# The issue order of an attention and state-space kernel, from a planner's ranks to one written list

## The chip, the cores and the metric

The kernel runs on one core of one Trainium2 chip. The metric is the device time of one execution in microseconds (us). A NeuronCore has five engines, each with an instruction stream of its own that is worked off strictly in order: PE (TensorE, matmul), DVE (VectorE), ACT (ScalarE), POOL (GpSimd) and SP (SyncE, which here only issues DMAs). Streams meet at semaphores. Matmuls write to PSUM, from which DVE or ACT must copy the result before the space can be used again.

## The reference

Two independent halves work on inputs of 2048 rows of 448 features, and their outputs stand side by side in a 2048 x 896 result.

```python
# A: sliding attention, 16 heads of 28, 8 keys at distances 0, 2, ..., 14 behind the query
qkv = x @ wqkv
logits = einsum("bhsd,bhswd->bhsw", q, k[idx]) * 28 ** -0.5      # idx = pos - 2 * (0..7), masked below 0
a = (einsum("bhsw,bhswd->bhsd", softmax(logits), v[idx])) @ wo
# B: diagonal state-space recurrence with 448 complex states
dt = exp(log_dt); Lam_bar = exp(dt * Lam); B_bar = ((Lam_bar - 1) / Lam)[:, None] * B
h[t] = Lam_bar * h[t-1] + B_bar @ x[t]
y = 2 * real(C @ h[t]) + x * Dskip
return concatenate([a, y], -1)
```

## The kernel before

Distances in the attention are even, so even and odd rows never meet; the kernel reads each input as 1024 pairs of rows. `xA` and `xB` hold the two x, transposed, as 7 blocks of 128 features (even rows, then odd rows) by 1024 pairs. The work is cut into some 518 named pieces ("nodes"). Each node is a Python function that emits a few instructions on one engine. These are the nodes that the text speaks of (lines of the kernel before):

- `xt0`, `xt1` (PE, L547): transpose the first 256 pairs of x; `xe..` (ACT or DVE) copy them to `xA`. The other blocks of x come by DMA transposes of SP (L311), `vw0` to `vw2` (DVE) build a second copy of the V weights, and `tr`, `pA`, `pB`, `pD`, `e1`, `e2`, `p2`, `p3a` are small parameter work (transposes of vectors, exponentials, sines).
- `wp10`, `wp11`, `wp00`, `wp01` (L555): copies of the K and Q weights into heads of 32 columns, two halves each; `pad` (POOL) zeroes the gaps between heads.
- `v0_`/`v0` to `v7_`/`v7` (PE): V of 128 pairs. A node of this kind uses the array as two tiles of 64 rows. The first half (`_`, 4 pairs of matmuls) and the second (3 pairs) swap tiles, and between them stands a relay, a one-element memset on POOL (`v0k`, L592) that waits for the first half and is waited for by the second. `ev0` copies the result out (ACT or DVE). `q{1,0}{s}{c}` (PE, L584/L585): K (1) or Q (0) of head group s and column chunk c (256, 256 and 512 pairs), in halves with relays like v; `eq...` copies out.
- `s{par}{b}` (PE, L782/L786): logits of query block b (9 blocks: 128 and then 112 pairs) for even or odd rows, four array tiles of 32 rows, two PSUM units; `x{par}{b}0`, `x{par}{b}1` (ACT, L792): the exponentials of the two units, written to one of three buffers `Pb`; `a{b}` (PE, L805): attention times V, which reads two of the `Pb` buffers; `n{b}` (DVE, L811/L812): reciprocal and normalising; `ot{b}` (SP, L818): DMA transpose of the result; `vi{b}` (SP, L737): two DMAs that build a window of V in the one buffer `vw`.
- `l1m`, `l2m`, `wtxm`: input weights of the recurrence, scaled on ACT/DVE and transposed by SP's DMA (L695). `xb1`: transposes of the second half of `xB`. `ctl` and `ctn..`: DMA transposes of C. `t0`, `tk`, `ts`, `t2`, `t3`, `t4`: tables of sine and cosine (`t2`, `t4` on ACT). `p3b0` to `p3b25`: small coefficient work on POOL. `cg..`, `ch..`: scaled copies of C (`C1`, `C2`). `dgE`, `dgO`: diagonal matrices on POOL. `gm..`, `zer..`, `one..`, `rcs`: masks and fills on POOL.
- `b{hf}{k}` (PE, L846): input of the states for half hf (512 pairs) and block k; `be` copies out; then on DVE `ma` (times tables, L857/L859), `ri` (L865 to L869), `sc` (scan, L875), `mb`, `ro` (L882 to L890).
- `g0`, `g1` (PE, L937): products of input weights with C1; `ge0`, `ge1` copy out. `y{t}`, `z{t}` (PE, L1038 to L1050): even and odd output rows of B for 128 pairs; for t >= 4 the Dskip part of z is added on DVE (`xd`, `ye..1`, L1075, from `xn`, a load of 560 KB). The last tile has z in two parts, `z70` of 320 and `z71` of 128 columns (L1056, L1084). `ye..` copy out, `yo..` store. `w{t}_`/`w{t}` (PE): attention output times wo, in halves with relays; `we..`, `wu..` copy and store; `wol` loads wo.
- `gu1` (DVE), `gu2` (PE), `gu3` (DVE): a check of the softmax sums that sets a flag; all engines read the flag at the end, and a branch to an exact second version of the attention follows (not taken).

PSUM is a pool of 4 units of two banks (`unit()`). A v, q, b, a, g, y, w node takes one unit, an s node two, z70 and z71 one each (other z share their y's). A unit comes free when its reader (`ev`, `eq`, `x`, `n`, `be`, `ge`, `ye`, `we`) is done. Buffers are bound when the functions run, in the order in which nodes are emitted, so this order also settles who waits for whom.

That order comes from a planner (`Plan`, L67 to L147). Each node has a cost per engine, dependencies, a rank (from `RANK` and `FINE`, L27 to L64) and the buffers that it takes and frees. `run` plays the schedule through in Python: whichever engine is free first takes the ready node of lowest rank (and, where a node may run on ACT or DVE, so chooses the engine); the nodes are emitted by start time. PE's order so made is:

```
xt0 xt1 v0_ v1_ v2_ v0 v1 v2 tr v3_ v4_ q101_ v3 v4 q111_ q101 q110_ q111 q100_ q110 q131_ q100 v5_ q131 q001_ q011_ v5 q000_ q001 q011 q000 q020_
q021_ v6_ q020 q021 v6 q010_ q121_ q130_ q010 q121 q130 q030_ v7_ q030 q122_ v7 q122 q120_ q031_ q032_ q120 q031 q032 s00 b00 s10 b01 s01 a0 q132_
q022_ q132 s11 q022 b03 s02 a1 b02 s03 q012_ q112_ q012 q112 s12 q002_ q102_ q002 q102 b13 a2 s13 b12 s04 a3 g1 s14 g0 s05 a4 b11 s15 b10 s06 a5 y0
s16 z0 y1 s07 z1 a6 s17 y2 z2 s08 w0_ w1_ w0 w1 s18 a7 y3 a8 z3 w3_ w2_ w3 w2 w4_ w5_ w4 w5 w6_ w7_ w6 w7 y4 z4 y5 z5 y6 z6 y7 z70 z71 gu2
```

SP's queue (behind the first loads of x and of the weights):

```
vi1 ctn0 wtx0 wtx4 ctn1 wtx1 wtx5 ctn2 wtx2 wtx6 ctn3 wtx3 xb1 ot0 ctl vi2 ot1 vi3 ot2 vi4 ot3 vi5 ot4 wol ot5 vi6 yo0 vi7 yo1 ot6 yo2 wu0 xn wu1 ot7
ot8 yo3 wu3 wu2 wu4 wu5 wu6 wu7 yo4 yo5 yo6 yo70 yo71
```

and the last nodes of all engines (P = PE, A = ACT, V = DVE, S = SP):

```
ye51:V yo5:S z6:P ye60:A y7:P ye61:V yo6:S z70:P ye70:A yo70:S z71:P ye71:V gu2:P ye72:V yo71:S gu3:V yo72:A
```

The buffer of exponentials goes by index: `P = h["P"] = Pb[i % 3]`, with i = 2b + par (L790 to L795).

Of the kernel before, what the change touches and what calls it, by code (L numbers as in the profile page):

```python
# [8 lines left out]
F32 = mybir.dt.float32  # L9
# [17 lines left out]
RANK = {"vi": (-982.65, 453.511), "v": (-387.88, 124.365), "q0": (-404.11, 174.618), "q1": (-2507.33, 507.753), "s": (-1342.93, 308.128), "a": (216.12, 576.185),  # L27
        "b0": (1545.63, 185.722), "b1": (11245.3, -469.953), "d0": (746.88, 309.32), "d1": (5554.67, -829.828), "l": (5955.06, 1367.61), "t": (1103.58, 127.088),
        "tk": (6422.82, -235.335), "xd": (6246.16, -577.448), "cg": (-5122.24, 262.931), "ch": (2931.32, -235.91), "g": (3436.98, -470.931), "y": (2815.64, 646.425),
        "w": (4665.11, 563.69), "gu": (9396.18, -1878.46), "q2": (3036.1, -233.616), "wp": (150.95, 837.504)}  # L30


FINE = {"t0": -79, "tk0": 102.8, "ts0": -64.1, "tk1": -2.2, "ts1": -79.4, "tk2": -301.1, "ts2": 32.8, "ts3": 239.6, "t3": 7.5, "t4": 332.3,
        "wp10": 11.6, "wp00": -475.4, "wp01": -41.6, "l10": 14.3, "l20": 53.7, "l14": -44.2, "l11": 28.9, "l21": 194.2, "l25": -117.2, "l12": -0.8,
        "l22": 127.9, "l26": 56.8, "l23": 202.6, "v0_": -64.5, "ev0": -345.5, "ev1": -264.2, "v2_": 10, "ev2": -165.8, "ev3": 331.4, "v4_": 346.3,
        "ev4": -1312.2, "v5_": -31.1, "ev5": 85.9, "v6_": -263.3, "ev6": -43.1, "v7_": 428.2, "ev7": -290.3, "vi2": -248.8, "vi3": -99, "vi4": 3.7,
        "vi5": -11.2, "vi6": -58.7, "vi7": 151.4, "q100_": -520.2, "eq100": -715.7, "q000_": -68.5, "eq000": 244.2, "q110_": -918.8, "eq110": -153.9, "q010_": 19,
        "q120_": 1076.7, "eq120": 175.4, "q020_": -1453, "eq020": 122.8, "q130_": 52.5, "eq030": 183.7, "q101_": 419.4, "q001_": -0.9, "eq001": -278.8, "q111_": -315.5,
        "eq011": 197, "q121_": 1063.8, "eq121": 43.8, "q021_": -8.9, "eq021": 99.9, "q131_": 9.3, "eq131": -535.8, "q031_": 460.5, "eq031": 131.2, "q102_": -370.6,
        "eq102": 21.6, "q002_": -191.7, "eq002": 155.7, "q112_": 30.8, "eq112": -413.6, "q012_": -48.7, "eq012": -454.3, "q122_": -790.4, "eq122": 1114.5, "q022_": 10.5,  # L40
        "q132_": 218.5, "eq132": 0.7, "q032_": 336.3, "eq032": 191.6, "s00": 0.8, "x000": -19.2, "x001": 411.7, "s10": 6.7, "x100": 2.4, "x101": 459.9,
        "a0": -246.8, "s01": -63.3, "x010": -294.8, "x011": 35, "s11": -334.8, "x110": -364.3, "x111": 1.8, "a1": -982.6, "n1": 569.6, "x020": -193.9,
        "x021": -4.1, "s12": 692.1, "x120": -76.2, "x121": 260.5, "a2": -593.1, "s03": -145.3, "x031": -671.6, "s13": 401.2, "x130": -16.7, "x131": 387.6,
        "a3": 363.9, "n3": -199.7, "s04": 154, "x040": -204.3, "x041": -248.6, "s14": -133.9, "x140": -49.4, "x141": -124.1, "a4": 16.5, "x050": 369.2,
        "x051": -21.2, "s15": 77.9, "x150": -716.7, "x151": -52.4, "a5": -437.2, "n5": -306.5, "s06": -46.9, "x061": -558.1, "x160": -137.5, "x161": -545.4,
        "a6": 178.3, "n6": 282.2, "s07": -91.9, "x071": -29.4, "x171": 99.3, "a7": 1425.2, "n7": 139, "s08": 122.4, "x080": -107.6, "x081": 203.1,
        "s18": 38.8, "x180": 522.3, "x181": 563.1, "a8": -371.4, "n8": -100.8, "b00": -49.1, "ma00": -53.7, "ri00": 49.5, "sc000": 11.2, "sc001": 488.3,
        "mb00": -17.9, "ro00": 132.3, "b01": -642, "be01": 173, "ma01": 194.6, "ri01": 170.3, "sc010": 45.7, "sc011": -244.2, "mb01": -173, "b02": 356.2,
        "ma02": 1465.7, "sc020": 27.4, "sc021": 332.5, "mb02": 358.9, "ro02": 105.2, "b03": 7.8, "ma03": 32.9, "ri03": -49.2, "sc030": 598.6, "mb03": 47.9,
        "ro03": -67, "b10": -44.5, "be10": 51, "ri10": 44.8, "sc100": -527.4, "sc101": 397.7, "mb10": 27.6, "ro10": -9.9, "b11": -200.8, "be11": -290.5,  # L50
        "ma11": 209.2, "ri11": -53.3, "sc110": 206.6, "sc111": -1655.3, "mb11": 42, "ro11": -62.6, "b12": 119.3, "ma12": -76.3, "ri12": 335.5, "sc120": 14.6,
        "sc121": -18.1, "mb12": 8.6, "ro12": -37.2, "b13": -342.4, "be13": 115.2, "ma13": -94.5, "ri13": 80.5, "sc130": -72.5, "mb13": -28.8, "ro13": -213.6,
        "cg10": 83.2, "cg20": -248.7, "cg11": -972.8, "cg21": 288.5, "cg12": -102.3, "cg22": -10.1, "cg23": -128.7, "cg14": 43.1, "cg24": 661, "cg15": -3.4,
        "cg25": -914, "cg16": 759.6, "cg26": -36.9, "ch20": -156.1, "ch11": -860, "ch21": 154.6, "ch12": 649, "ch22": -66.3, "ch13": -177.8, "ch23": -699.3,
        "ch14": -124.5, "ch15": 95.4, "ch25": -264, "ch16": -11.2, "ch26": -302.4, "g0": 150.9, "ge0": -200.9, "g1": -328.9, "ge1": -140.7, "gu1": -15.8,
        "gu3": -239.5, "xd4": 107.8, "xd5": 31.3, "xd6": -336.2, "xd7": -178.6, "w0_": 798.9, "we0": -195, "w1_": 357.4, "we1": 258.7, "w2_": 819.4,
        "we2": 33.6, "w3_": -157.3, "we3": -87.8, "w4_": -79.5, "we4": -255.6, "we5": 74.8, "w6_": -427.9, "we6": 295.2, "w7_": 478.1, "we7": -221.9,
        "y0": -43, "z0": 282.6, "ye0": -555, "y1": -175.8, "y2": 590.7, "z2": -494.1, "ye2": -182.2, "y3": 1111.2, "z3": 63.5, "y4": -26.3,
        "z4": -325.5, "ye41": 15.1, "y5": -451.9, "z5": 56.9, "ye50": 201, "y6": -497.6, "z6": 11.4, "ye60": 477.6, "ye61": 662.1, "y7": -39.3,
        "z70": 37.4, "ye71": -540.7, "z71": 89.3, "ye72": -535.8, "tk3": -279, "t2": -17, "wp11": -97.5, "l24": 156.9, "l15": -58.9, "l16": 54.8,  # L60
        "l13": 19.1, "v1_": -32.2, "v3_": 60.8, "eq130": -37.6, "q030_": -118.8, "eq101": 124.2, "eq111": -763.1, "q011_": -79.2, "n2": -113.6, "x030": 43.8,
        "n4": -6.3, "x060": 39.8, "s16": -1.8, "x070": -50.2, "s17": -21.9, "x170": 4, "be00": -279, "ro01": -191.8, "be02": 110.2, "ri02": -1.9,
        "ma10": -0.8, "be12": 5.9, "cg13": -368.5, "ch10": 22.5, "ch24": 105.9, "gu2": 376.5, "w5_": 2, "z1": -10.3, "ye3": -30.9, "ye40": -35.3,
        "ye51": -13.1, "ye70": 399.5}  # L64


class Plan:  # L67


    WAKE, TURN = 0.18, 0.1  # L70

    def __init__(self, pools):
        self.nodes, self.pools = [], pools

    def add(self, name, cost, fn, deps, rank, alloc=None, n=1, frees=(), at=0.0, lat=0.0, mode="f"):
        d = dict(name=name, cost=cost, fn=fn, deps=list(deps), rank=rank, alloc=alloc, n=n, frees=list(frees), at=at,
                 lat=lat, mode=mode, end=None, by=None)
        self.nodes.append(d)
        return d

    def ready(self, n, e):
        t = n["at"]
        for d in n["deps"]:
            if d["end"] is None:
                return None
            w = d["end"] + d["lat"] + (self.WAKE if d["by"] != e else 0.0)
            t = w if w > t else t
        p = n["alloc"]
        if p:
            r = self.ring[p]  # L90
            for k in range(len(r), len(r) + n["n"]):
                k -= self.pools[p]
                if k >= len(r):
                    return None
                if k >= 0:
                    if r[k]["left"]:
                        return None
                    t = max(t, r[k]["end"] + self.WAKE)
        return t

    def run(self, clock):
        left = sorted(self.nodes, key=lambda n: n["rank"])
        self.ring = {p: [] for p in self.pools}
        for n in left:
            n["units"] = [dict(left=0, end=0.0) for _ in range(n["n"])] if n["alloc"] else []
        for n in left:
            for a, j in n["frees"]:
                a["units"][j]["left"] += 1
        clock, mode, order = dict(clock), "f", []
        while left:  # L110
            e = min((e for e in clock if any(e in n["cost"] for n in left)), key=lambda e: clock[e])
            now, best, soon = clock[e], None, None
            for n in left:
                if e not in n["cost"]:
                    continue
                t = self.ready(n, e)
                if t is None:
                    continue
# [26 lines left out]
        for n in order:  # L145
            n["fn"](n["by"])
# [986 lines left out]
```

## Time and profile before

| | us |
|---|---|
| median of 9 runs (lowest to highest) | 133.82 (133.62 to 134.0) |
| the profiled execution, device time | 133.63 |
| its span, first to last instruction | 131.9 |
| PE busy / DVE / ACT / POOL | 124.9 / 107.4 / 87.1 / 27.8 |
| granted TensorE clock, mean | 0.995 |

The profile is one execution on the chip. The rows of tenths cut the span into 40 slices of 3.3 us. A row of the timeline gives start, duration, engine, line, operation, output and input; in brackets stand the engine's idle time ahead of it and what ended that. A row of the waits gives the total, the number and the longest of one kind of wait. Matmuls are pipelined: the recorded duration of one (0.38 us for 512 columns) overlaps the next, which starts 0.22 us later. The rate at which PE advances is therefore read from starts, not from durations.

### The profile page before, as it was taken

How to read it: one execution, taken by the hardware profiler on the slowest of the kernel's cores; microseconds unless marked ns; L12 is line 12 of the kernel's file. 1: busy time of each engine (PE TensorE's matmuls, PEld its weight loads, DVE VectorE, ACT ScalarE, POOL GpSimd, SP SyncE). 2: the span in 40 equal slices, each digit the busy share in tenths (PEclk: the TensorE clock that was granted, in tenths of full speed). 3: DMA queues.
4: the chain of work that ended last, by engine and by line, in shares of the span. 5: the costliest groups of instructions: out<-in, count | busy, mean ns of one | idle time of the engine just before them, and what ended most of it. 6: DMA issues, size and time to landing. Idle time of an engine off the chain costs nothing.

```text
span 131.9 us, 3802 instructions
## 1 busy us (share of the span) xinstructions
PE 124.9 (95%) x1529; PEld 70.7 (54%) x1529; DVE 107.4 (81%) x187; ACT 87.1 (66%) x115; POOL 27.8 (21%) x109
## 2 busy tenths in 40 slices
PE   5899998999979999999999999999999999999980
PEld 2445966977434545445555644655656655455550
DVE  0619989999869799999999999999999999941140
ACT  3519998797995694899998948774759334511110
POOL 6985155103830397000000000000000000000000
PEclk9999999999999999999999999999999999999997
DMA  3999998979888999352238025492252888542231
GB/s 93 318 269 253 140 264 191 141 170 127 162 157 160 158 193 117 80 120 35 75 62 136 0 77 61 127 252 72 74 134 81 243 151 203 182 139 75 70 102 50
DMA packets 43681, 18.18 MB, mean 138 GB/s; under 512 B 33660, under 2 KB 43644, under 8 KB 43660
## 3 DMA queue, kind: packets, MB, share of 16 engines
q1 hardware_dynamic: 42992, 17.47, 63.8%
q10 hardware_dynamic: 572, 0.38, 0.9%
q8 instruction: 13, 0.21, 0.7%
q14 instruction: 8, 0.07, 0.2%
q0 software_dynamic: 96, 0.06, 0.1%
HBM read 4.99 MB, written 3.67 MB: 66 GB/s over the span
## 4 chain that ended last, share of the span: by engine, by line
PE 77%; SPq 7%; DMA 5%; ACT 4%; DVE 3%; issue 2%
PE mm L584 23%; PE mm L846 14%; PE mm L1038 8%; PE mm L1045 7%; PE mm L805 6%; DMA xA<-in_A_x_dram 5%; PE mm L1040 5%; PE mm L937 4%; PE mm L782 4%; SPq L311 3%; PE mm L786 2%; PE mm L585 2%; ACT P L792 1%; DVE Wp L555 1%; ACT L792 1%
## 5 line engine op out<-in xcount | busy, mean ns | idle before, releaser
L792 ACT ACTIVATE P<-mm 128x896 bf16<-128x896 f32 (+1 forms) x36 | 31.6, 932 | 3.5 <-PE mm L786 3.5
L584 PE MATMUL mm<-xA,Wp 64*128 64x256 bf16 (+1 forms) x168 | 26.5, 305 | 0.5 <-DVE Va L563 0.5
L585 PE MATMUL mm<-xA,Wp 64*128 64x256 bf16 (+1 forms) x168 | 26.5, 305 | 0.0
L561 ACT CAST ys<-mm 128x896 bf16<-128x896 f32 (+1 forms) x14 | 11.0, 801 | 19.5 <-PE mm L1045 8.9
L846 PE MATMUL mm<-xB,WT 128*128 128x512 bf16 x98 | 22.5, 379 | 0.3 <-ACT P L792 0.3
L592 POOL MEMSET tick<- 1x1 f32 x40 | 4.4, 110 | 82.8 <-PE mm L585 82.6
L584 PEld LDWEIGHTS <-Wp 64*128 64x128 bf16 x168 | 15.4, 94 | 6.6 <-POOL tick L592 0.3
L585 PEld LDWEIGHTS <-Wp 64*128 64x128 bf16 x168 | 15.2, 94 | 1.0 <-issue 0.8
L846 PEld LDWEIGHTS <-WT 128*128 128x128 bf16 x98 | 9.0, 98 | 11.2 <-issue 1.1
L584 PE MATMUL mm<-Wv,xA 64*128 64x448 bf16 x56 | 12.2, 350 | 0.1
L585 PE MATMUL mm<-Wv,xA 64*128 64x448 bf16 x56 | 12.2, 350 | 0.0
L1038 PE MATMUL mm<-C,h 128*128 128x448 bf16 x56 | 11.9, 353 | 0.0
L584 PE MATMUL mm<-wo,OT 64*128 64x448 bf16 x56 | 10.9, 349 | 0.0
L585 PE MATMUL mm<-wo,OT 64*128 64x448 bf16 x56 | 10.9, 349 | 0.0
L1045 PE MATMUL mm<-C,h 128*128 128x448 bf16 x49 | 10.4, 353 | 0.0
L561 ACT CAST u<-mm 128x1024 bf16<-128x1024 f32 (+1 forms) x7 | 6.2, 891 | 6.0 <-PE mm L846 6.0
L812 DVE TENSOR_TENSOR O<-mm,rcs 112x896 bf16<-112x896 f32 (+1 forms) x9 | 9.8, 1092 | 0.3
L875 DVE TENSOR_TENSOR_SCAN rs<-p_r,ini,rv 128x512 bf16<-128x512 f32 x7 | 8.6, 1269 | 0.0
L805 PEld LDWEIGHTS <-P 128*128 128x128 bf16 x288 | 8.1, 96 | 1.0
L875 DVE TENSOR_TENSOR_SCAN rs<-p_r,rv 128x512 bf16<-128x512 f32 x7 | 8.5, 1228 | 0.0
L1075 DVE TENSOR_TENSOR ys<-mm,xd 128x448 bf16<-128x448 f32 x3 | 1.9, 625 | 7.3 <-ACT ys L561 7.3
L584 PEld LDWEIGHTS <-OT 64*128 64x128 bf16 x56 | 5.1, 94 | 5.0
(171 smaller groups left out, 241.3 us busy)
## 6 DMA issues: line engine op xcount, KB each, us to landing
out_dram<-ys SPq DMA_DIRECT2D x15, 224.0 KB, 2.4
Wkr<-in_A_wqkv_dram SPq DMA_DIRECT2D x2, 336.0 KB, 3.7
Wqr<-in_A_wqkv_dram SPq DMA_DIRECT2D x2, 336.0 KB, 4.6
wo<-in_A_wo_dram SPq DMA_DIRECT2D x2, 336.0 KB, 3.1
P<-in_A_x_dram SPq DMA_DIRECT2D x2, 224.0 KB, 3.4
xo<-in_B_x_dram SPq DMA_DIRECT2D x1, 448.0 KB, 3.7
vw<-Va SPq DMA_DIRECT2D x2, 203.0 KB, 2.8
vw<-Va SPq DMA_DIRECT2D x2, 174.0 KB
```

The lines of the kernel that those rows point to most:

```text
L561: ACT.copy(o, i)
L584: x = PE.matmul(ps[:, a, 0:n], lhs(0, lo[i]), rhs(0, lo[i]), start=(i == 0), stop=(i == 6), skip_group_check=True)
L585: y = PE.matmul(ps[:, b, 0:n], lhs(64, hi[i]), rhs(64, hi[i]), start=(i == 0), stop=(i == 6), skip_group_check=True)
L782: PE.matmul(at(g)[:, 0:4 * n].rearrange("p (s q) -> p s q", s=4), msk[32 * g:32 * g + 32, 0, :], msk[32 * g:32 * g + 32, 1:2, c0:c0 + n].t ...
L792: ACT.activation(P[:].rearrange("p s g q -> p g s q")[:, 2 * z:2 * z + 2, :, 0:n], h["s"][z][:, :, 0:4 * n].rearrange("p g (s q) -> p g s ...
L805: PE.matmul(av[:, par, 29 * hd:29 * hd + 29], hb_[par]["P"][:, hd // 4, hd % 4, :], v[:, par, hd, :], start=True, stop=True)
L812: V.tensor_tensor(O[0:n, :].rearrange("p (a h d) -> p a h d", a=2, h=H), avv[0:n, :, :, 0:DH], rc.unsqueeze(3).to_broadcast((n, 2, H, DH)) ...
L846: PE.matmul(ps[:, i, :], WT[:, j, 128 * m:128 * m + 128], xB[:, j, HALF * hf:HALF * hf + HALF], start=(j == 0), stop=(j == 6))
L875: V.tensor_tensor_scan(h["s"][:, i], p["r2"][:, k:k + 1].to_broadcast((128, HALF)), h["v"][:, i], 0.0 if hf == 0 else ini[:, m:m + 1], ALU ...
L1038: PE.matmul(ps[:, 0, 0:D], hb[:, m, lo:lo + 128], lazy["C2"][:, m, :], start=(m == 0), stop=False, skip_group_check=True)
L1040: PE.matmul(ps[:, 0, 0:D], xB[:, k, tk], Gm[:, k, :], start=False, stop=(k == 3), skip_group_check=True)
L1045: PE.matmul(ps[:, 1, 0:D], hb[:, m, lo + 1:lo + 129], lazy["C1"][:, m, :], start=(m == 0), stop=(t in YD and m == 6), skip_group_check=True)
```

## The change

The planner, its ranks and its costs in use go; what is left of `Plan` calls the nodes in the order of a list `ORDER`, which names for each node its engine. All arguments on dependencies, ranks and buffers are still written at the nodes but no longer read (many costs there are changed, and play no part). The instructions of a node are the same, but for these: a new node `tl` on ACT behind `t4`; the buffer of exponentials is taken in the order of use; `gu2` may stand anywhere; the store `yo71` goes to ACT. The engine of some nodes differs from the planner's choice, for instance `wp..` and `be00` are on DVE, `ev5`, `ev7`, `eq022`, `eq002` and `we2` on ACT.

```diff
+ORDER = """
+eye:G xt0:P xe00:A xe01:A iot:G gm0:G xt1:P xe11:A gm1:G vw0:V vw1:V vw2:V v0_:P v0k:G v2_:P xe10:V tr:P pA:V e1:A v0:P v2k:G ev0:A pD:V v2:P ev2:A
+pB:V t0:A pad:G wp11:V wp10:V v1_:P v1k:G gm2:G v3_:P v1:P ev1:V v4_:P wp00:V wp01:V ctn0:S v3k:G v3:P ev3:A tk0:V tk1:V q131_:P gm3:G v4k:G v4:P
+q131k:G ev4:A q131:P eq131:A gm4:G gm5:G q110_:P q110k:G q100_:P q100k:G q101_:P q101k:G q110:P eq110:A q100:P eq100:A q000_:P gm6:G q101:P eq101:V
+ts0:V v5_:P e2:A p3a:V ts1:V p2:V l10:V tk3:V l14:V l20:V wtx0:S l24:V wtx4:S ts3:V q000k:G q000:P eq000:A v6_:P gm7:G v5k:G v5:P ev5:A q111_:P v6k:G
+v6:P gm8:G ev6:A q020_:P q111k:G q111:P eq111:A q001_:P zer2:G q020k:G l13:V tk2:V l23:V q020:P eq020:A ts2:V gm9:G q001k:G q120_:P q120k:G q010_:P
+q010k:G zer0:G q001:P eq001:A q011_:P q011k:G gm10:G q120:P eq120:A q010:P eq010:A ctn1:S q031_:P q011:P eq011:A q030_:P wtx3:S q121_:P l11:A l21:V
+q031k:G q031:P eq031:A v7_:P gm11:G q030k:G q121k:G l15:A l25:V wtx5:S q030:P eq030:A t2:A q021_:P q121:P eq121:V l12:V l16:V ctn2:S wtx1:S v7k:G v7:P
+ev7:A q122_:P one1:G t3:V q130_:P q021k:G zer1:G q021:P eq021:A q122k:G q122:P eq122:V q130k:G l22:V wtx2:S q130:P eq130:V gm12:G b00:P gm13:G l26:V
+gm14:G zer3:G one0:G xb1:S ctn3:S be00:V s00:P q032_:P q032k:G rcs:G p3b0:G p3b1:G t4:A ma00:V ri00:V tl:A x000:A x001:A p3b2:G p3b3:G p3b4:G p3b5:G
+p3b6:G s10:P x100:A q032:P eq032:A p3b7:G p3b8:G x101:A b01:P be01:A a0:P s11:P x110:A sc000:V sc001:V mb00:V x111:A n0:V b03:P be03:A s01:P x010:A
+ro00:V ma01:V q022_:P q132_:P p3b9:G q022k:G q022:P x011:A eq022:A q132k:G ri01:V sc010:V q132:P sc011:V mb01:V ro01:V eq132:A s02:P x020:A x021:A
+vi1:S wtx6:S b02:P be02:A ma03:V ri03:V a1:P n1:V ctl:S p3b10:G p3b11:G p3b12:G p3b13:G p3b14:G p3b15:G p3b16:G p3b17:G p3b18:G s12:P x120:A sc030:V
+mb03:V ro03:V q012_:P q012k:G x121:A ma02:V ri02:V sc020:V sc021:V s03:P q012:P eq012:A q112_:P q002_:P p3b19:G p3b20:G p3b21:G x030:A x031:A q112k:G
+q112:P eq112:A q102_:P p3b22:G q002k:G vi2:S q002:P eq002:A p3b23:G q102k:G q102:P eq102:A p3b24:G s13:P a2:P p3b25:G cg10:V cg20:V n2:V x130:A x131:A
+b13:P s04:P ch12:V cg13:V ch22:V cg23:V be13:A ma13:V ri13:V x040:A x041:A cg15:A ch10:A dgE0:G vi3:S dgO2:G b10:P be10:A ch20:V ot1:S ot0:S cg25:V
+a3:P s14:P n3:V cg16:V cg26:V cg14:A cg24:V x140:A x141:A ch14:V ch24:V b12:P s15:P be12:A cg12:A cg22:V cg11:V vi4:S b11:P x150:A x151:A ot2:S be11:A
+a4:P ch13:V cg21:V ch23:V ch11:V n4:V ch15:A ch21:V mb02:V ro02:V ch25:V ch16:V s05:P x050:A x051:A ch26:V dgE1:G dgE2:G dgO0:G dgE3:G dgO3:G dgO1:G
+g0:P ge0:A g1:P ge1:A vi5:S a5:P n5:V s16:P y0:P x160:A x161:A s06:P z0:P x060:A x061:A y1:P sc130:V ma12:V ri12:V ye0:A mb13:V ro13:V ot4:S sc120:V
+s17:P x170:A x171:A vi6:S wol:S ot5:S z1:P sc121:V mb12:V ye1:A ot3:S a6:P ro12:V vi7:S s07:P x070:A x071:A ma11:V n6:V ot6:S y2:P z2:P ye2:A ri11:V
+sc110:V sc111:V s08:P x080:A x081:A w0_:P w1_:P w0k:G w0:P we0:A w1k:G w1:P we1:A s18:P mb11:V ro11:V yo0:S a7:P n7:V ot7:S y3:P x180:A x181:A a8:P
+z3:P ye3:A ma10:V n8:V xn:S ot8:S w3_:P w3k:G w4_:P wu0:S yo1:S yo2:S w4k:G w5_:P ri10:V w3:P w4:P we3:A w5k:G w5:P w6_:P gu1:V sc100:V sc101:V mb10:V
+ro10:V w2_:P we4:A w7_:P we5:V w6k:G w6:P we6:V w2k:G w2:P w7k:G wu6:S we2:A wu1:S xd4:V xd6:V w7:P y6:P ye60:A y5:P we7:A z6:P y7:P z5:P xd7:V ye61:V
+wu2:S yo3:S wu5:S wu3:S wu4:S wu7:S y4:P yo6:S ye50:V xd5:V ye51:V yo5:S gu2:P z70:P gu3:V ye40:A ye70:A ye71:V yo71:A z4:P ye41:V yo70:S z71:P ye72:V
+yo4:S yo72:A
+""".split()
...
+    def run(self):
+        left = dict(self.nodes)
+        for w in ORDER:
+            name, e = w.split(":")
+            cost, fn = left.pop(name)
+            assert e in cost, w
+            fn(e)
+        assert not left, left
...
+    def n_tl(e):
+        ACT.activation(t_([1, 1], F32, "tl"), hpi[0:1, :], ACTF.Exp)
+
...
+    tl = node("tl", {"A": 1.5}, n_tl, [t4], ("t", 0))
...
-                P = h["P"] = Pb[i % 3]
+                if z == 0:
+                    h["P"] = Pb[npb[0] % 3]
+                    npb[0] += 1
+                P = h["P"]
...
-                node(f"yo{t}{1 + i}", {"SA"[i]: 0.5}, put, [n3], 61 + i + 3 * t, lat=2.2)
+                node(f"yo{t}{1 + i}", {"A": 0.42}, put, [n3], 61 + i + 3 * t, frees=[(n2, 0)], lat=2.2)
...
-    plan.run({"P": 4.3, "A": 4.5, "V": 1.0, "S": 25.2, "G": 3.15})
+    plan.run()
```

In the list the letter G is POOL. GpSimd's masks, fills and coefficient work (`gm`, `zer`, `one`, `p3b`, `dg`) stand in it between the relays (names that end in k), one or a few behind each.

## The prediction

> **What bounds it now.** I read the page first (busy times, the 40 slices), then the waits of PE, then the PE timeline, in which I measured each piece of work as the distance from its first matmul to the first matmul of the next piece.
>
> ```profile
> span 131.9 us, 3802 instructions
> PE 124.9 (95%) x1529; PEld 70.7 (54%) x1529; DVE 107.4 (81%) x187; ACT 87.1 (66%) x115; POOL 27.8 (21%) x109
> ...
> PE   5899998999979999999999999999999999999980
> ...
> DVE  0619989999869799999999999999999999941140
> ```
>
> PE's row is full from the second slice to the last but one, and DVE's is full from slice 14 to 35 (43 to 115 us). So PE sets the end, but it cannot run far ahead of DVE. An order can win only PE's stalls; the matmuls stay the same.
>
> ```profile
> PE mm L547 <- DMA P<-in_A_x_dram: 0.6, 1, 0.6
> PE mm L584 <- DVE Va L563: 0.5, 1, 0.5
> PE mm L782 <- ACT P L792: 0.4, 1, 0.4
> PE mm L846 <- ACT P L792: 0.3, 1, 0.3
> ```
>
> These waits are few, and they understate the loss, because a pipelined matmul counts as busy until its modelled end. The distances give more. Up to `v5_` at 16.95 us PE follows the first loads of x (block 5 lands at 16.90), and neither those loads nor the work that precedes `v5_` (11.5 us in both lists) changes. From 16.95 to the end of `z71` at 128.03 us pass 111.08 us. The medians of the distances are v 0.76 + 0.57, q of 256 columns 0.44 + 0.33, q of 512 columns 0.86 + 0.65, s 0.50, a 0.82, b 3.03 (1.52 for k = 3), g 2.78, y 2.08, z 1.53 or 1.32, w 0.76 + 0.57, z70 0.95, z71 0.48; each change between full, half and quarter tiles adds 0.09 (a 0.82 before y, 0.90 before q). Laid end to end in the old order they make 108.94. **So 2.14 us of stall is all there is to win**: 0.64 at `q020_` (the row "DVE Va" above), 1.22 around `s10` and `b01`, 0.19 at `g1`, the rest in crumbs. The second is seen here:
>
> ```profile
> 37.12 0.39 PE L782 MATMUL mm<-msk 32*128 32x512 bf16 x2
> 37.93 0.39 PE L782 MATMUL mm<-msk 32*128 32x512 bf16 x2 [0.42 <-ACT P L792]
> 37.94 0.61 PE L786 MATMUL mm<-Qt,Kt 28*128 28x128 bf16 x16
> 38.84 0.38 PE L846 MATMUL mm<-xB,WT 128*128 128x512 bf16 x1 [0.30 <-ACT P L792]
> ```
>
> The second half of `s10` and then `b01` wait for the first two exponentials, since each of them empties a PSUM unit.
>
> **The new order, laid end to end.** It has 43 tile changes where the old one has 44 (-0.09), and `gu2` (0.16) moves from behind `z71` to ahead of it. From 16.95 that makes 109.01, so `z71` would end at 125.96 without waits. Against 128.03 that is a gain of 2.07. Now the waits. The rule, from rows of before: PSUM has four units, so a piece waits for the reader of the unit taken four allocations earlier. A reader starts about 0.17 after the next piece's first matmul, and the writer follows 0.05 after the reader's end.
>
> *Q and K phase (to 31 us).* The old stall at `q020_` goes: `ev5` is now on ACT (0.91 for DVE's 1.07) and `wp01` (1.64 at 18.86) is no longer ahead of it. I walked every unit with the readers' rows (ACT 0.59, pitch 0.48; DVE 0.69): the margins are 0.1 to 0.9 us. The projection copies `wp10`, `wp11` move from ACT (1.50 each) to DVE (0.62 and 1.64 are its two rows) into DVE's idle 7 to 10 us and a little after; at worst 3.3 us, done by 13.6 where `q110_` needs them at 13.9. Cost 0; if they slip, `v5_`'s load still covers about 0.3.
>
> *First exponential.* `b00` now wants its two transposed weight blocks at 31.3 (and 32.8); they are first in SP's queue, at 26.9 and 28.3, and took 3.0 to 4.6 us to land before: 0 to 0.25, I take 0. `b00` (3.12) is ahead of `s00`, and `tl` (an exponential of one element) loads the table under it. `t4` ends at about 33.4, a load is 1.28, e1-like work 0.20: 34.95 (0.20 is `e1`'s row), and `s00`'s readers start at 35.10. The trace shows no lone exponential in this place; between 0 and 0.3 I take 0. Then `s10`: its second half needs `x000`, 35.10 + 1.02 + 0.05 = 36.17, against 35.97: **0.2**, where 1.22 was.
> The page "ScalarE: Activation LUTs", section "What ACT_TABLE_LOAD costs", puts a switch of sets at about 2.66 us, 1.28 of load and 1.38 of drain. The trace has the load (35.56 to 36.84) and the exponential 0.01 behind it, so no drain; by the page `s10` would stall 1.2 longer.
>
> *DVE against PE.* `be00` is now on DVE and starts at 34.48 (before: 37.22). Behind it come 16 pieces up to `n1`, without rest: 1.33 + 1.26 + 0.68 + 2.36 + 1.22 + 1.41 + 1.08 + 1.26 + 0.70 + 1.22 + 1.25 + 1.26 + 0.88 + 0.72 + 0.88 + 1.37 = 18.9, from the distances on DVE between 37 and 59 us, and 0.1 for `a0`. Two of them:
>
> ```profile
> 43.53 0.36 DVE L811 RECIPROCAL rcs<-mm 128x32 f32<-128x32 f32 x1 [0.71 <-PE mm L805]
> 43.93 1.09 DVE L812 TENSOR_TENSOR O<-mm,rcs 128x896 bf16<-128x896 f32 x1
> ```
>
> So `n1` ends at 53.46. It empties `a1`'s unit, and `s03`, only two pieces behind `a1`, takes that unit: 53.50 for 52.93, **0.55**. Were DVE free, it would still be 0.2 (0.17 + 1.41 + 0.05 against 1.45 of PE work); with DVE 0.3 slower, 0.9.
>
> *Short distances on ACT.* `q002_` takes the unit of `q012`, with only `q112_` (0.86) between. Before, two pieces lay between (0.81 + 0.50) and it just fitted:
>
> ```profile
> 56.23 1.01 ACT L561 CAST Qt<-mm 128x1024 bf16<-128x1024 f32 x1 [0.34 <-PE mm L585]
> 57.14 1.02 ACT L561 CAST Kt<-mm 128x1024 bf16<-128x1024 f32 x1
> ...
> 57.30 0.37 PE L584 MATMUL mm<-xA,Wp 64*128 64x512 bf16 x1
> ```
>
> 56.03 to 57.30 is 1.27; less 0.86 is **0.41**. The same chain of casts makes `b13` **0.1** late. And the ring of three by use gives `x130` the buffer that `a2` reads, so it starts after `a2`; `s04`'s second half needs `x131`: 0.17 + 0.82 + 0.92 + 0.05 = 1.96 against 1.7: **0.25**. Elsewhere the ring's reuse follows its reader by at least one piece, as before.
>
> *From 64 us.* The walk finds no further wait: `g0` comes 1.2 us or more behind its last constant, `y0` 1.4 or more, `ro10` ends at about 112.2 and `y6` wants it at 113.7, though `gu1` (1.29) now stands ahead of it on DVE. SP: `vi1` is moved behind six weight transposes and `xb1`; it would land at 45.5 and `a1` wants it at 50.6. Every later window has over 2 us. `we7` must wait for the store `wu1` to free its staging buffer (about 118), but the next taker of its unit, `y4`, comes at 122.6. I add 0.2 for crumbs (before had 0.3). **Waits: 0.2 + 0.55 + 0.41 + 0.1 + 0.25 + 0.2 = 1.7; bounds 0.8 and 2.6.**
>
> *GpSimd.* Of the relays' waits only 0.3 us ever reached PE's weight loads. In both orders a second half follows its first by 0.57 or more, and a relay needs about 0.16 + 0.09 + 0.1. The placement of the small work is worth nothing either way, unless it hits DVE: the second `wp01` copy took 1.64 beside three GpSimd memsets, the first 0.62, and a table product 1.31 beside the masks for 1.22. Bounds 0 and 0.6 on the way to `n1`; I take 0.
> "SBUF — State Buffer" (section on its two physically separate sides) calls the pair of ports that VectorE and GpSimd share an exclusive lock for a whole instruction. If it held, each of some ten small operations (0.2 each) beside `be00` to `n1` could hold up DVE, up to 2 us, and `s03` with it; the row 1.31 says far less.
>
> **The end.** Before, the last things are a piece of 128 columns (`z71`) and a 32 KB store. Now `z4` (448 columns) is last but one, with its add of 0.62 and a store of 224 KB:
>
> ```profile
> 127.75 0.69 DVE L1084 TENSOR_TENSOR ys<-mm,xd 128x320 bf16<-128x320 f32 x2 [1.80 <-PE mm L1056]
> ...
> 128.27 0.34 SPq L1087 DMA_DIRECT2D out_dram<-ys  x1
> ...
> out_dram<-ys SPq DMA_DIRECT2D x15, 224.0 KB, 2.4
> ```
>
> From the last matmul's end (128.10) the span goes on for 3.80. SP's closing semaphore waits stand in the trace one after the other, 0.07 each; the last but one of the stores' is at 130.28, and 1.62 follow. Now this one is `yo4`'s. With E for the last matmul's end: add done E + 0.31, issue E + 0.34, landing 2.37 later, E + 2.71, and 1.62 more: 4.33. **+0.53** (bounds 0.2, if SP does not wait for it, and 0.9).
>
> **Sum**, against the profiled execution (133.63, span 131.9 and 1.73 around it): -2.07 + 1.7 + 0.53 = +0.16, 133.8. That execution lies 0.19 under the median of 133.82. **I forecast 134.0**, no change that can be told (0.2%, 0.27 us, is about what a measurement of this kernel can tell).
>
> **Rivals.** (1) *The waits at 50 to 63 us don't come.* DVE had 0.7 us idle before `n0` and 1.4 before `be00`; if its chain is shorter by 0.6 and SP's end does not wait for `yo4`, 0.8 of waits and 0.2 at the end are left: -1.07, **132.8** (132.3 to 133.4). For it: PE and ACT have room almost everywhere. Against: DVE's rows are all back to back already.
> (2) *A transpose is late.* `ot8` feeds `w7_`. It is issued at about 105.7, 1 us behind the load of `xn` (560 KB). Before, the transpose behind that load took 5.9 us (103.87 to 109.79), the next 3.1. `w7_` comes at 111.2, so beyond 5.5 us each microsecond counts in full: 0.4 to 1.4 on top, **134.9**. DVE slower by more than 0.3 adds to the same side.
> (3) *The change of GpSimd's order does nothing*: that is my sum already.
>
> **Chances.** The walk as it stands 0.45 (its own range 133.6 to 134.5), rival 1 0.33, rival 2 0.22. Of the walk a tenth is faster by over 0.2%, half within, the rest slower. Faster 0.37, same 0.22, slower 0.41. The range reaches over most of rival 1 and half of rival 2: 132.6 to 134.9.
>
> **What would show it.** In the new trace: no wait at `q020_`; a table load that ends before `s00` does; PE waiting at L782 for DVE O (about 53 us), at L584 for ACT Qt (55.6) and at L782 for ACT P (63); `z71` ending near 127.7; SP ending 4.3 us behind it. It is wrong if DVE rests before `n1`, if PE stalls after 64 us, or if the end takes 3.8.

## The result, and the profile after

The changed kernel takes 134.96 us (median of 10 runs, 134.72 to 135.99), the kernel before 133.78 beside it: ratio 1.010, 95% interval 1.0082 to 1.0118. It is slower by 1.0%. The forecast was 134.0, the range ended at 134.9. The times of the changed kernel fall in two groups, 134.7 to 135.0 and 135.7 to 136.0; those of the kernel before do not.

The page of the changed kernel (busy times and the 40 slices; its profiled execution took 135.57, one of the upper group):

```profile
span 133.8 us, 3795 instructions
PE 125.7 (94%) x1529; PEld 70.3 (53%) x1529; DVE 104.9 (78%) x192; ACT 85.1 (64%) x111; POOL 39.0 (29%) x109
...
PE   6899989999999999899999999999999999999940
...
DVE  0458495989999999999998995999999899801630
```

PE's row is full in nearly every slice, and yet the span is longer: the last but one slice is emptier than before (4 for 8). I cut both executions at the two points that the prediction uses, the start of `v5_` and the end of the last matmul of `z71`:

| us | before | after | predicted | measured |
|---|---|---|---|---|
| span's start to `v5_` | 16.95 | 17.68 | 0 | +0.73 |
| `v5_` to the end of `z71` | 111.15 | 110.84 | -0.37 | -0.31 |
| end of `z71` to the span's end | 3.82 | 5.24 | +0.53 | +1.42 |
| span | 131.92 | 133.76 | +0.16 | +1.84 |

So the middle, with nearly all of the work and nearly all of the prediction's working, came out as foretold. What failed lies at both ends, most of it behind the last matmul. Of the head's 0.73 little is left in the medians (they differ by 1.18, and the two lower rows make 1.11); the experiments come back to it.

The waits of PE in the changed kernel (us in total, times, longest):

```profile
PE mm L511 <- DMA xA<-in_A_x_dram: 0.5, 1, 0.5
PE mm L704 <- DVE O L737: 0.4, 1, 0.4
...
PE mm L511 <- ACT Qt L488: 0.2, 1, 0.2
```

The first is `v5_` waiting for block 5 of x, the second `s03`, the third `q002_`. The old waits for DVE Va and for ACT P are gone from the list (`PE mm` is a matmul, and the name behind the arrow is what it waited for). The timeline about the first exponentials (start, duration, engine, line):

```profile
34.50 1.28 ACT L559 ACT_TABLE_LOAD   x1
...
35.26 0.40 PE L704 MATMUL mm<-msk 32*128 32x512 bf16 x4
...
35.80 0.20 ACT L559 ACTIVATE tl<-p_hpi 1x1 f32<-1x1 f32 x1
...
35.96 2.86 ACT L717 ACTIVATE P<-mm 128x1024 bf16<-128x1024 f32 x3
...
36.78 0.65 PE L704 MATMUL mm<-msk 32*128 32x512 bf16 x4
```

The table is loaded while PE works on `b00`, and the exponential follows it without a pause. `s10` (36.78) is only 0.26 longer than its work, where `s10` and `b01` stalled 1.2 before. And about `n1` and `s03`:

```profile
53.22 1.09 DVE L737 TENSOR_TENSOR O<-mm,rcs 112x896 bf16<-112x896 f32 x1
...
54.37 0.37 PE L704 MATMUL mm<-msk 32*128 32x448 bf16 x4 [0.38 <-DVE O L737]
...
56.79 0.37 PE L511 MATMUL mm<-xA,Wp 64*128 64x512 bf16 x1 [0.24 <-ACT Qt L488]
```

By distances the waits are 0.46 at `s03` and 0.41 at `q002_`. The end of the changed kernel:

```profile
127.97 0.55 PE L981 MATMUL mm<-C,h 128*128 128x128 bf16 x7
128.22 0.62 DVE L1000 TENSOR_TENSOR ys<-mm,xd 128x448 bf16<-128x448 f32 x1 [0.89 <-PE mm L970]
...
128.88 0.54 SPq L989 DMA_DIRECT2D out_dram<-ys  x1
129.08 0.38 ACTq L1014 DMA_DIRECT2D out_dram<-ys  x1
```

The store of 224 KB (`yo4`) is issued 0.36 behind the last matmul's end, as foretold (0.34). It lands at 131.69, and the 32 KB store behind it (`yo72`) at 132.17: SP's closing wait for it ends at 132.19, and 1.57 follow. Before, the same 32 KB took 1.6, and both last stores had landed (129.88, 130.04) when SP came to its waits for them (130.28, 130.35): there SP's own row of waits set the end, here a landing does.

### The profile page after: what moved, and what is told of

The parts are those of the page before. It is cut to its first block, busy times and chain, and to the rows that moved or that the text cites. A ratio compares the mean times of both kernels' runs of the same rounds, so it can differ in the third digit from the quotient of the medians.

```text
span 133.8 us, 3795 instructions
## 1 busy us (share of the span) xinstructions
PE 125.7 (94%) x1529; PEld 70.3 (53%) x1529; DVE 104.9 (78%) x192; ACT 85.1 (64%) x111; POOL 39.0 (29%) x109
## 4 chain that ended last, share of the span: by engine, by line
## 5 line engine op out<-in xcount | busy, mean ns | idle before, releaser
L488 ACT CAST ys<-mm 128x896 bf16<-128x896 f32 (+1 forms) x13 | 10.4, 822 | 19.0 <-PE mm L965 8.5
L488 ACT CAST Qt<-mm 128x512 bf16<-128x512 f32 (+1 forms) x12 | 8.8, 730 | 2.9 <-PE mm L512 2.7
```

The lines of the kernel that those rows point to most:

```text
L488: ACT.copy(o, i)
```

## Experiments

All times are medians; "before" is the kernel before on the same chip. Edits are to the issue list (P = PE, V = DVE, A = ACT, G = POOL, S = SP); "old list" is the order of the kernel before, written as a list in the changed code, with `tl` behind `t4`. A profile's head, middle and end are the three stretches of the table above; the end is counted from the end of `z71` also where `gu2` stands behind it.

**Old list alone** (the control for the experiments on it).

> The old list as an explicit list, with tl behind t4; no other change. Both theories: 133.7 to 134.0, v5_ at 16.9 to 17.3, the end 3.7. Rival: tl moves the table load out of the way of the first exponential also here and wins up to 1.2: 132.6.

Measured: 133.92 (before 133.80, ratio 1.001, 0.9998 to 1.0022); middle as before, end 3.81, and the stall at `s10` and `b01` still there (1.24). `tl` is worth nothing by itself: in the old list `s00` is done before `t4` ends at 35.66, so the load starts right behind `t4` with `tl` (35.68) as without (35.56 before).

**The old end, first try.**

```diff
-gu2:P z70:P gu3:V ye40:A ye70:A ye71:V yo71:A z4:P ye41:V yo70:S z71:P ye72:V yo4:S yo72:A
+gu2:P gu3:V ye40:A z4:P ye41:V yo4:S z70:P ye70:A yo70:S ye71:V yo71:S z71:P ye72:V yo72:A
```

> The changed list with the end of the old one: z4 and its 224 KB store go back ahead of z70, yo71 goes back to SP; gu2 stays ahead. Theory E (the end is the mis-sized term: 5.2 us from the last matmul to the end of the span for 3.8, the store yo4 and the small store yo72 behind it): from z71's end 3.8 to 4.1 us again, the median 133.5 to 133.9, 1.1 to 1.4 below the changed kernel's 134.96. Rival W (the waits before 64 us cost more than the sum says, and the end is worth the 0.53 of the prediction): 134.4 to 134.6. Rival H (the loads of x land 0.7 us later because of the new order, and v5_ with them): the head stays late, v5_ at 17.7 in the profile, and 134.2 or more.

Measured: 135.47 (1.0135, 1.0112 to 1.0157), slower than the changed kernel. All three theories missed. My edit made a wait of its own (`z4` right behind `y4` waits 0.57 for `ye40`), but the end was still 5.04 long, although the last stores were small. That spoke against the 224 KB store as the whole cause.

**The new end on the old list.** From `y6` on the order of the changed list.

> The old list up to the last four output tiles, and behind it the new end: y6, y5, z6, y7, z5, y4, gu2, z70, z4, z71, with yo71 on ACT. Theory E: the old 133.8 plus 1.44 for the end, less 0.16 for gu2, 134.9 to 135.2. Rival W: plus 0.53 less 0.16, 134.1 to 134.3. Rival H says the same as W.

Measured: 135.99 (1.0161, 1.0146 to 1.0175), 2.07 above the old list alone and above what either theory said; the end is 5.74. The end alone costs more than the whole change.

**`n1` ahead of `ri03`.**

```diff
-be02:A ma03:V ri03:V a1:P n1:V
+be02:A ma03:V a1:P n1:V ri03:V
```

> The changed list with one swap on DVE: n1 (empties the PSUM unit that s03 takes) ahead of ri03 (0.70). The wait of s03 (0.46 in the profile) goes and nothing else moves: 134.5, 0.3 to 0.5 below the changed kernel. If instead DVE's total is what bounds PE there, the wait comes back at a later piece and the time stays at 134.9 to 135.0.

Measured: 136.10 (1.0181, 1.0148 to 1.0214), 1.1 above the changed kernel, where the same time or a gain was expected. The wait at `s03` shrank to 0.19, but PE's waits now have this row:

```profile
PE mm L771 <- DVE O L737: 0.8, 1, 0.8
```

It is `b10` (0.88 by distance), which takes the unit that `n2` empties. DVE waited 0.67 for `a1` before `n1`, and its row is without rest from there to `n2`: the pause on DVE comes back at `b10`. The middle is 111.45, longer by 0.6; the rest of the 1.1 is not accounted for. DVE's total up to `n2` bounds PE here.

**Second half of `q012` ahead of `s03`.**

```diff
-s03:P q012:P eq012:A q112_:P q002_:P
+q012:P eq012:A s03:P q112_:P q002_:P
```

> The changed list with one swap on PE: the second half of q012 ahead of s03. It runs in the time in which s03 waits for n1, and its eviction eq012 starts earlier, so that q002_ finds its unit empty: both waits (0.46 and 0.41) go in one, 134.1 to 134.3. If the second half's relay is not done in time, or ACT holds eq012 behind x121, only one of them goes: 134.5. If DVE's total bounds PE there: 134.9.

Measured: 134.76 (1.0087, 1.0059 to 1.0114). Both waits went, 0.39 came for the relay, and `b10` waits 0.31 for `n2`: middle 110.57. So the two waits were one idle moment of PE, and DVE took a part of the gain back. The 134.1 to 134.3 of the first theory were not reached.

**The same with `n2` ahead of `cg10` and `cg20`.**

> The changed list with the second half of q012 ahead of s03, and on DVE n2 ahead of cg10 and cg20 (1.15 us, constants of the product g0, which has room). With q012 alone PE won 0.87 before s03 and q002_ (less 0.39 for the relay) and lost 0.31 at b10, which waits for n2, the last of DVE's row without rest. Theory D (DVE's row up to n2 bounds PE at b10): b10 no longer waits, v5_ to the last matmul 110.25 for 110.57 and 110.84, median 134.4 to 134.5. Rival: DVE's total bounds PE all the way to y6, so that a later piece waits instead: 134.7 to 134.8, as with q012 alone.

Measured: 134.52 (1.0069, 1.0044 to 1.0094), middle 110.27, no wait at `b10`.

**The old end, `y7` late.**

```diff
+y6:P ye60:A y5:P we7:A z6:P y4:P z5:P ... ye40:A z4:P gu2:P gu3:V ye41:V yo4:S y7:P
+z70:P ye70:A yo70:S ye71:V yo71:S z71:P ye72:V yo72:A
```

> The changed list, and its end in the old manner: z4 (whole tile, 224 KB store) directly behind y4 and z5, then y7, z70, z71, so that the last store but one is issued some 2 us before the last matmul's end; yo71 on SP. In the experiment before it, z4 stood directly behind y4 and waited 0.57 for ye40, and three stores were crowded on SP. Theory E (the 224 KB store behind the last matmul makes the end 5.24 long): the end is 3.7 to 3.9 again, no new wait, median 133.4 to 133.7. Rival: the end is long for another reason (SP's flag load, the number of stores on ACT's queue): 134.5 or more.

Measured: 134.71, from 133.65 to 135.94 (1.0053, 1.0026 to 1.0081). So the rival held. In the profile the end is 4.04. Of the same end in the next run it is 5.33: `yo71` of 80 KB lands 3.50 behind its issue there and 2.14 here. So the end varies by 1.3 with no 224 KB store behind the last matmul.

**Both.**

> Both: the old end and the two swaps. Both theories: the gains add up, 132.8 to 133.1, faster than the kernel before (133.8) by 0.5 to 0.8%. If the gain in the middle is lost at the end (DVE late for the last additions): 133.4 to 133.7.

Measured: 134.10, from 133.04 to 135.44 (1.0006, 0.9978 to 1.0034): a microsecond above the 132.8 to 133.1 of both theories, and no longer slower than the kernel before.

What the three ends have in common with the changed one, and not with the kernel before, is `gu2` ahead of `z70`. The changed kernel's trace has PE load the flag and branch at 2.14 and 1.27 us *ahead* of the last matmul's end. The lines of the branch (PE's sequencer; shortest/median/longest in ns, then first and last start), after and before:

```profile
L1027 PEldq COMPARE_BRANCH  x1: 398/398/398, 127.3 to 127.3; - x1
...
L1101 PEldq COMPARE_BRANCH  x1: 398/398/398, 129.1 to 129.1; - x1
```

Then one transfer of 16 KB on queue 8 (instructions) runs from 0.13 ahead of the last matmul's end to 0.93 behind it. In the kernel before PE branches 0.93 behind the last matmul, and the 16 KB move at 2.06 to 3.43 behind it, when the stores have landed. The next runs test this.

**`gu2` last.**

```diff
-gu2:P z70:P gu3:V ... z71:P ye72:V yo4:S yo72:A
+z70:P ... z71:P gu2:P ye72:V gu3:V yo4:S yo72:A
```

> The changed list with gu2 and gu3 (the one-row product of the error flag) behind z71 again, as in the kernel before; everything else as changed, z4 and its 224 KB store still late. Theory Q (in the changed kernel PE loads the flag and branches at 2.1 and 1.3 us ahead of the last matmul's end, and the 16 KB of instructions that the branch fetches move from 0.1 us before it to 0.9 behind it, on the DMA engines that the last stores need; before, the fetch came 2.1 to 3.4 behind it): the fetch is again over 1.5 us behind the last matmul, the store of 32 KB lands in 1.6 to 2.0 us for 3.1, the end is 4.2 to 4.5 for 5.24, median 134.0 to 134.3. Rival S (the 224 KB store ahead of it in the queues is what delays the 32 KB store): the fetch moves, the store still takes 3 us, the end stays at 5.1 to 5.3, 135.0 or more.

Measured: 134.41 (134.04 to 135.93; 1.0073, 1.004 to 1.0105; before 133.98). The excess over the kernel before falls from 1.18 to 0.43 in the medians; the intervals of the two ratios still overlap, since the late heads are in both. The end is 4.55 for 5.24; the prediction's step for it gives 4.33. DMA in the changed kernel, 127.9 to 130.3 (queue with packets, MB, share; then stores with KB and us to landing):

```profile
q8 instruction: 1, 0.02, 2.8%
...
out_dram<-ys SPq DMA_DIRECT2D x1, 224.0 KB, 2.8
out_dram<-ys ACTq DMA_DIRECT2D x1, 32.0 KB, 3.1
```

With `gu2` last, 127.2 to 129.6:

```profile
out_dram<-ys SPq DMA_DIRECT2D x1, 224.0 KB, 2.5
out_dram<-ys ACTq DMA_DIRECT2D x1, 32.0 KB, 2.4
```

The small store lands 0.7 earlier, and that is what the end gains; it is not back at the 1.6 to 2.0 that theory Q named.

**`gu2` early, alone, on the old list.** One move, no 224 KB store near the end.

```diff
-z70:P ye70:A yo70:S z71:P ye71:V gu2:P ye72:V yo71:S gu3:V yo72:A
+gu2:P gu3:V z70:P ye70:A yo70:S z71:P ye71:V ye72:V yo71:S yo72:A
```

> The old list with one change: gu2 and gu3 ahead of z70 instead of behind z71. The prediction's step: PE ends 0.16 earlier, 133.6. Theory Q: the fetch moves into the last stores and the end grows by 0.3 to 1.6, median 134.1 to 135.2. Rival S: 133.6 to 133.7.

Measured: 135.65 (1.0139, 1.012 to 1.0158; before 133.98). This one move costs 1.7 us; the end is 5.16 and has 1.35 of it. DMA about the end in the kernel before, 127.5 to 130:

```profile
q1 hardware_dynamic: 444, 0.32, 39.9%
q10 hardware_dynamic: 144, 0.03, 5.9%
issues: line engine op xcount, KB each, median us to landing
...
out_dram<-ys SPq DMA_DIRECT2D x1, 80.0 KB, 1.6
out_dram<-ys ACTq DMA_DIRECT2D x1, 32.0 KB, 1.6
```

The old list with `gu2` early, 128 to 130.4:

```profile
q8 instruction: 1, 0.02, 4.0%
...
out_dram<-ys SPq DMA_DIRECT2D x1, 80.0 KB, 3.3
out_dram<-ys ACTq DMA_DIRECT2D x1, 32.0 KB, 3.2
```

The same, 130.4 to 133:

```profile
q14 instruction: 3, 0.02, 3.8%
q1 hardware_dynamic: 9, 0.01, 1.7%
q10 hardware_dynamic: 9, 0.00, 0.4%
```

The same two stores take 3.2 us for 1.6. Their bulk moves as fast as before, but nine packets of each are left over, of 144: one sixteenth, the share of one of the core's 16 DMA engines. The fetch holds 129.37 to 130.93, and the leftover packets move from 130.91 to 131.63, with and behind three fetches of 8 KB on queue 14. In 12 of the 13 profiles with `gu2` early the last eight data packets of one store stand still like this and start within 0.03 us of the 16 KB fetch's end; in the thirteenth (the first try of the old end) they start at the end of an 8 KB fetch. That fetch and share wait for the same engine is read from these times; the records do not name the engine.

The changed kernel is not fully explained by this. There the held share is that of `yo71` (issued at 127.37, its last eight data packets from 129.44 on, the fetch ending at 129.45). The last packets of the two last stores end at 131.11 and 131.15, as soon behind their issue (2.23 and 2.07) as with `gu2` last (2.09 and 2.02). But they count as landed 0.58 and 1.02 behind their last packet, for 0.36 and 0.39. Why stays open; two fetches of 8 KB (131.15 to 131.46, 131.55 to 131.93) lie just ahead of the two landings.

**The old end, the two swaps, and `gu2` last.**

> The old end, the two swaps in the middle, and gu2 last. Theory Q: the end is 3.7 to 3.8 as in the kernel before and no longer different from run to run (5.33 and 4.04 in two profiles of the same end with gu2 early); v5_ to the last matmul 110.3 to 110.4; median 132.7 to 133.1, faster than the kernel before by 0.5 to 0.8%. Rival S: gu2 costs 0.16 and brings nothing, 134.1 to 134.3.

Measured: 133.27 (132.53 to 134.41; 0.9945, 0.9913 to 0.9977), for 1.0006 with `gu2` early; here the intervals are apart. The end is 3.53, and the median a little above the 133.1 of theory Q. But the spread stayed, and here is why, in this execution's waits of PE:

```profile
PE mm L511 <- DVE Wp L482: 1.3, 1, 1.3
```

The last part of the q weights landed at 16.95, in other profiles from 14.1 on. The copy `wp00` on DVE waits for it, `q000_` for the copy, and the new list has `q000_` ahead of `v5_`, the old one behind it.

**Without `tl`.**

> The changed list without the exponential of one element (tl); it feeds nothing. Theory D (DVE's row without rest bounds PE from 34 to 64 us): the first exponential starts 0.15 to 0.2 earlier, the wait behind s10 (0.26) shrinks, s03 waits longer by as much, and the time stays at 134.9 to 135.0. Rival: ACT is the bound there and 0.15 is won: 134.8. A second rival: the table load then falls on the first exponential and costs over 1 us: 136.

Measured: 136.49 (1.0193, 1.0177 to 1.0208). The second rival holds: the load now stands behind the wait for `s00`,

```profile
36.92 1.28 ACT L717 ACT_TABLE_LOAD   x1 [2.23 <-PE mm L708]
```

and `s10` waits 1.53. (`b00` also waits 1.04 for its weights in this execution.) In the new list `tl` is worth over 1 us; theory D was wrong here, since a stall of that size is more than DVE's row gives.

**GpSimd's small work in its new places, alone, on the old list.**

> The old list with GpSimd's small work in the new places behind the relays (the ones for the window copies stay where they were); nothing else changes. The prediction's step: worth nothing, 133.7 to 133.9. Rival: it holds up DVE or the relays, and part of the loss is here: 134.1 or more.

Measured: 135.86 (1.0154, 1.0134 to 1.0173), the middle is longer by 2. PE's waits:

```profile
PE mm L511 <- POOL tick L519: 1.9, 2, 1.3
```

Behind the relay that is first in the new list another one is due at once in the old: `q022k` stood behind nine `p3b` (45.46 to 48.51) and came 1.3 late. The places are not worth nothing. They fit one order of PE only, and the changed kernel has no such wait.

**The head.** In five profiles of old heads `v5_` starts at 16.95 to 17.34, in ten of new ones at 16.98 to 18.53. The remaining runs are on it. First, more work ahead of `v5_`:

> The changed list with one piece, the first half of q111, moved from behind v6 to ahead of v5_ (0.44 of PE work that needs no late block of x). Theory X (the new list has no stall left between v5_ and the first exponentials, so each late landing of x block 5 goes to the end in full; ten profiles of new lists show v5_ from 16.98 to 18.53): v5_ starts at 17.1 to 17.2 unless block 5 lands later, q020_ 0.3 to 0.45 earlier where it lands late, median 134.5 to 134.8 and a smaller spread. Rival R (the late head is the profiled execution alone, the executions that are timed have none): 134.9 to 135.0.

Measured: 135.41 (1.0115, 1.0091 to 1.0138), a miss for both: block 5 landed at 17.40, `v5_` began at 17.45, and `b00` waited 0.52 for its weights. Then block 5 made late on purpose, `for i in (6, 5, 7)` for `range(5, 8)`:

> The changed list, with the loads of x blocks 5 and 6 swapped in SP's queue, so that block 5 lands about 0.75 later. Theory X: all of it goes to the end, 135.5 to 135.9. Rival R: nothing or little of it, 134.9 to 135.2.

> The old list (with tl behind t4) and the same swap of the loads of x blocks 5 and 6. Theory X: the stall of 0.64 at q020_, which waits for the eviction ev5 and so for v5, moves with block 5, and what is left of the delay meets the 1.22 at s10 and b01, which hangs on ACT: 0 to 0.3 above the old list. Rival: the old list pays 0.75 as well, 134.4 to 134.7.

Measured: 135.48 (1.013, 1.011 to 1.0149) on the new list, and 134.66 on the old (1.0064, 1.0048 to 1.008; 0.74 above the old list alone, `v5_` at 17.93). Theory X falls: the old list pays in full as well, because everything up to `b01` moves along with `v5_`. Last, the late loads taken away:

```diff
     xbar_x(xA, xA2, 512, 640)
+    xbar_x(xA, xA2, 640, 768)
     w_load(0)
-    for i in range(5, 8):
+    for i in range(6, 8):
```

with `q000` and `q111` changing places in the list, and `wp00`, `wp01` behind `eq101`.

> The changed list with block 5 of x loaded ahead of the q weights instead of behind them; so that nothing waits for those instead, the pieces q000 and q111 change places in the list (q111 needs the k weights alone), and on DVE tk0 and tk1 go ahead of eq101 and the copies wp00 and wp01 behind it. Theory L (what makes the head late and the times of new lists spread is the landing of x block 5 and of the q weights behind a queue of loads, 15.6 to 17.9 and 14.1 to 17.0 in the profiles): v5_ starts at 16.6 to 16.9 in every execution, the upper group of times at 135.8 to 136.0 goes, median 134.5 to 134.8. Rival: the spread has another cause, two groups remain.

Measured: 135.04, from 134.91 to 135.16 (1.0088, 1.0075 to 1.0101). Block 5 lands at 12.4, `v5_` starts at 17.08 behind nothing but PE's own work, and in five executions there is no upper group. The lower group is not beaten, and the expected 134.5 to 134.8 are missed: `b00` gives back 0.29, waiting for its weights.

> The same head before the version with the old end, gu2 last and the two swaps in the middle (133.27 against 133.98 for the kernel before on its chip). Theory L: 132.5 to 132.9, with a spread of 0.6 or less, faster than the kernel before by 0.7 to 1.0%. Rival: 133.0 to 133.4 and the old spread of 1.9.

Measured: 132.88, from 132.73 to 133.17 (0.993, 0.9916 to 0.9944), 0.7% faster than the kernel before and the best of all. Its page:

```profile
span 131.2 us, 3797 instructions
...
PE 125.3 (96%) x1529; PEld 70.2 (53%) x1529; DVE 104.8 (80%) x192; ACT 85.2 (65%) x111; POOL 37.3 (28%) x109
```

## Why the prediction was wrong, point by point

- **"So 2.14 us of stall is all there is to win", gain 2.07, waits 1.7.** Right. In the profile the waits behind `v5_` are 1.76 (-0.31 for the middle less the -2.07 without waits): `s10` 0.26 (0.2 predicted), `s03` 0.46 (0.55), `q002_` 0.41 (0.41), `b13` 0.09 (0.1), `b00` 0.13 (0 to 0.25), `a5` 0.28 (0.19 of it stood at the same place before), crumbs. The wait at `s04` (0.25) did not come, and `a5` stalls behind 64 us, where the walk found nothing; such misses cancel, so the total is nearer than its parts. DVE from the start of `be00` to the end of `n1` took 18.95, where 18.9 were worked out. (`be00` was on DVE before, too, at 37.22, and not only now, as the text ahead of the prediction and the prediction say; no term hangs on it.) The middle gained 0.31, and 0.37 was foretold.
- **"`z71` ending near 127.7"**: 127.8, once the late head is taken off.
- **"`gu2` (0.16) moves from behind `z71` to ahead of it."** This is the step that failed. The prediction priced the matmul (109.01 is 108.94 - 0.09 + 0.16) and put what hangs on it at nothing: the flag, each engine's load of the flag, the branch, and the instructions fetched behind the branch. They ran beside the last stores. Alone on the old list the move costs 1.7 us for the 0.16; putting it back takes 0.69 off the changed kernel's end and 0.75 off its excess. (The expectations that take 0.16 off for an early `gu2` have the sign of this term wrong.) Behind the rows: the Trainium skill, "Runtime: NRT & Kernel Launch", section "Instruction fetch mechanics", says that instructions come in blocks of 16 KiB by DMA and that a taken branch whose target is not at hand forces a fetch. The trace agrees on the size (one transfer of 16384 bytes, 0.96 to 1.55 us, from 1.1 us behind PE's branch in every profile with `gu2` early); whether the branch counts as taken it does not show.
- **"The end +0.53", by `yo4`'s store.** Near for what it counted: with `gu2` last the new end takes 4.55, where 4.33 was worked out (the store lands 2.45 behind its issue, 2.37 was taken, and the 32 KB store lands 0.16 behind it and is waited for last). That is +0.73, inside the bound of 0.9. With `gu2` early it is 5.24, +1.42. The upper bound was too low because it knew only the store.
- **"Those loads ... and the work that precedes `v5_` ... unchanged", `v5_` at 16.95.** The work is; the landing is not a constant. Block 5 of x landed from 15.6 to 17.9 in the profiles, and the one profile of before happened to have 16.90. 3 of the 10 executions of the changed kernel are 0.9 longer than the rest, and with the late loads taken away none of 5 is, and in the version with the old end the range falls from 1.88 to 0.44: the last two runs show that these loads cause the spread.
- **"The placement of the small work is worth nothing either way."** True of the change as a whole, wrong as a reason: small operations ahead of a due relay can hold PE up (nine of them by 1.3 us in the experiment).
- **`tl` at 0.** I credited its gain to `b00`; the run without it shows that the two work only together. Behind the load nothing more came (0.02 between load and `tl`), so the row of before was right for this place.
- **The port that VectorE and GpSimd share.** The Trainium skill, "SBUF — State Buffer", section "SBUF: two separate sides", calls it an exclusive lock for the whole instruction, and up to 2 us were weighed for that. They did not come on top: 18.95 for 18.9. But the rows that made the 18.9 had run beside GpSimd as well (busy 8.9 us from 35.3 to 54.4 before, 11.3 after), so no run here tells whether there is such a lock.
- **Rivals.** None held. The waits came (against 1), `ot8` was in time (against 2: no stall behind 64 us but `a5`), and slower came by the end.

Why late loads are seen in heads of new lists more often than of old ones (mean landing of block 5 about 17.3 in ten profiles, 16.6 in five) stays open. The queue of loads is the same in both, and so few executions may mislead.

## What to carry to other kernels

Price an instruction that is moved by all that it releases: here a flag led to a branch, the branch to instruction fetches, and where they met the last stores the end grew, by 1.35 us in the run that moved nothing else. Where two engines are both near full, a wait taken off one comes back at the next buffer that the other empties, so look for the end of the full engine's row before paying for a swap. And one profile gives one landing time of a load: where PE stands right behind a load, take a range.

## What was not expected of the hardware

- PE reads the flag and branches while its own last matmuls still run: the branch began 1.27 us ahead of the last matmul's end.
- A fetch of 16 KB takes 0.96 to 1.55 us as one transfer. In the old list with `gu2` early it holds one sixteenth of the packets of the two last stores, and they land 3.3 and 3.2 us behind their issue for 1.6.
- The same DMA issue on SP (`yo71`) takes 0.34 us in the kernel before and, beside the fetch, 0.89 and 1.24 in the two versions with `y7` late.
- Block 5 of x, behind the same queue of loads, landed from 15.6 to 17.9 us.
